# Windowed attention and a gated layer on one core: a change of order, of pairing and of the dilated heads' layout

## The chip, the core and the metric

The kernel runs on one core of a Trainium2 chip. The core has five engines that each take their own list of instructions in order: TensorE (PE) multiplies matrices into eight PSUM banks, VectorE (DVE), ScalarE (ACT) and GpSimd (POOL) work on elements, and SyncE (SP) issues transfers between memory and the core. An instruction that waits holds up all that stands behind it on its engine. The metric is the device time of one execution, in microseconds, lower is better.

## What is computed

```python
# q, k, v: 8 batches x 8 heads x 576 tokens x 64
scores = q @ k.T / sqrt(64)
mask_plain = (rel >= 0) & (rel < 32)                      # heads 0 to 3; rel = row - column
mask_dil   = (rel >= 0) & (rel < 128) & (rel % 4 == 0)    # heads 4 to 7
attn = softmax(where(mask, scores, -1e9)) @ v
x = attn with the heads side by side                      # 4608 tokens x 512
h = x @ w_in                                              # 512 x 1024
e = exp(h - max(h)); sm = e / sum(e); solu = h * sm
ln = (solu - mean) / sqrt(var + 1e-6) * g_ln
out = ln @ w_out                                          # 1024 x 512
```

## The kernel before

A unit is two heads of one batch (32 units, four to a batch; the third and fourth of each batch are dilated). The host puts the dilated heads' tokens class by class (token modulo 4), so that their mask becomes a plain window inside a class. For a unit n, the words `S` (scores, 72 small matmuls), `mask`, `max`, `sub`, `exp`, `sum`, `inv`, `norm` and `turn` make the transposed weights, and `V` multiplies them with the values into PSUM. `xh` (or `xf`) copies the result, rounded, into `x_hi`; `xl` (or `xd`) puts the rest into `x_lo`; where POOL forms the rest, `xc` first makes a plain copy for it. These copies put a dilated unit's tokens back into their order.

A tile is 128 tokens (36 tiles). Every product with `w_in` and `w_out` is done in two parts: high times high, high times low, low times high, so that one block of 128 rows costs three matmuls. For tile i the words `ha`, `hb` (left half of the columns) and `hc`, `hd` (right half) are six matmuls each; `ha` and `hc` need the units 0 and 1 of the batch, `hb` and `hd` the units 2 and 3. Then `peak` (DVE), `e` (ACT), `gate` (DVE), `mid`, `var` make the normalised row, `forth` and `back` send it through memory and back, `tr`, `th`, `tl` turn and split it, and `o` (24 matmuls; `oA` and `oB` are its halves) makes the output, `out` scales and stores it. The tiles' products with `w_in` stand in banks 0 and 1 or 2 and 3; the outputs of the early tiles in banks 0 and 1, which are free for them when the gate of tile 4 is done.

From tile `PAIRED` on two tiles go together: seven products `P1` to `P7` of six matmuls (42) take the place of eight blocks (48), with sums `z1` to `z4` of their inputs, and of the weights (`fa` to `fh`, then `Th`, `Tl`), made beforehand. `s` and `c` put the products together, `pk` finds the peak.

The two weight matrices come as 64-bit numbers, 16 blocks of 0.52 MB, and are turned into two rounded parts on the chip: for block b, `w` loads it, `field`, `low` and `sign` take the number apart, `join` puts it together, `hi` and `lo` make the two parts. Blocks 0 to 7 are `w_in`, 8 to 15 `w_out`; `hc` needs the blocks 1 and 3, `ha` 0 and 2, `hb` 4 and 6, `hd` 5 and 7.

The order is written out by hand: `OPENING` is a list of words, each of which issues its instructions on its engines; the loop after it does the same with `PAIR_BODY` for the last pairs. Each engine runs its own instructions in the order of that list. Tables say which engine does a step: `PE_MASK` (units whose mask is added by two matmuls of PE before the scores, line 307, rather than by DVE at line 337; these units' `sub` is on DVE, line 355, the others' on POOL, line 358), `POOL_NORM`, `DVE_LOW`, `ACT_CENTRE` (`mid` on ACT or DVE), `ZERO_SIGN` (`sign` on ACT or DVE), `ON_DVE` (`tl` and weight sums on DVE rather than POOL).

Of the kernel before, what the change touches and what calls it, by code (L numbers as in the profile page):

```python
# [21 lines left out]
NPAIR = H // 2  # L22
# [18 lines left out]
PE_MASK = (0, 1, 2, 3, 4, 5, 6, 7, 8, 9)  # L41
POOL_SUB = True
POOL_NORM = (0, 1, 2, 3, 4, 5, 6, 7, 8, 9, 10, 11, 12, 14, 15, 21, 22, 23, 25)
ACT_SCORES = ()
POOL_X = (2, 4, 5, 6, 9)
DVE_LOW = (0, 4, 8, 9, 10, 11, 12, 14, 15)
ACT_CENTRE = (0, 3, 4, 5, 7, 9, 10, 11, 14, 15, 20, 21)
# [3 lines left out]
ZERO_SIGN = (1, 2, 4, 5, 6, 8, 9, 10, 11, 12, 13, 14)  # L51
OPENING = (
# [87 lines left out]
def pair_words(r):  # L140
# [15 lines left out]
    "var.b tlA.a tlB.a out.d by.b tlA.b tlB.b oE.a out.a "  # L156
    "oE.b outE.b "
)
PAIRED = 12
SPLIT_UNIT = 16  # L160
POOL_WORDS = "z1 z2 z3 z4 lS12 lS34".split()
LOWEST = -3.4e38
# [12 lines left out]
def windowed_attention_then_solu_kernel(  # L175
# [70 lines left out]
    def buf(n):  # L246
        return n % 4 if n < 12 else n % 2
# [837 lines left out]
```

## Time and profile before

| | |
|---|---|
| median of three runs | 499.30 us (499.17 to 500.08) |
| profiled execution | 496.32 us |
| its span, first to last instruction | 494.5 us |
| PE busy | 461.7 us, 93% |
| DVE, ACT, POOL busy | 346.9, 306.6, 256.0 us |
| mean granted clock of TensorE | 0.997 |

The span is what the profile covers; 1.8 us of the execution lie outside it. PE is busy nearly throughout after the first 90 us; before, all of it, the loads, the conversion of the weights and the first units stand in each other's way. A matmul's end is modelled, so that PE's busy time in the opening contains waiting.

### The profile page before, as it was taken

The page shows a single profiled execution, that of the slowest core. Times are in us where ns is not written, and L with a number is a line of the kernel's source. Part 1 is how long each engine was busy: PE and PEld are TensorE (multiplying, and loading weights), DVE is VectorE, ACT ScalarE, POOL GpSimd, SP SyncE. Part 2 cuts the span into 40 slices and gives each one's busy share as a digit, 9 for nine tenths or more (in the row PEclk, how much of TensorE's full clock was granted, in tenths as well). Part 3 has the DMA queues.
Part 4 walks back from the last instruction along what each step waited for, and adds up shares of the span by engine and source line. Part 5 has one row for each costly group of instructions (what it writes and reads, how often), then busy time and mean ns, then how long its engine had stood idle before and what let it go on. Part 6 is the DMA issues. An engine that isn't in the chain of part 4 may idle for free.

```text
span 494.5 us, 15618 instructions
## 1 busy us (share of the span) xinstructions
PE 461.7 (93%) x6604; PEld 372.4 (75%) x6604; DVE 346.9 (70%) x622; ACT 306.6 (62%) x503; POOL 256.0 (52%) x334
## 2 busy tenths in 40 slices
PE   2469988899999899999999999999899999999996
PEld 1356766778887688788878888878688888888885
DVE  2867977877989467788959776867476754445472
ACT  4779877745652544574766666566566677667552
POOL 0245444734440546989448441676465656766420
PEclk9999999999999899999999999999999999999999
DMA  8978755774843435666488565866745545354452
GB/s 303 345 276 307 222 168 143 215 243 140 260 119 129 138 104 183 187 188 232 147 246 242 175 191 184 228 211 196 259 133 162 161 133 157 102 162 137 107 168 88
DMA packets 50902, 92.58 MB, mean 187 GB/s; under 512 B 5648, under 2 KB 25616, under 8 KB 50832
## 3 DMA queue, kind: packets, MB, share of 16 engines
q1 hardware_dynamic: 50112, 90.92, 59.1%
q8 instruction: 52, 0.85, 0.7%
q10 hardware_dynamic: 720, 0.66, 0.4%
q14 instruction: 18, 0.15, 0.1%
HBM read 58.53 MB, written 28.31 MB: 176 GB/s over the span
## 4 chain that ended last, share of the span: by engine, by line
PE 87%; DMA 4%; DVE 3%; ACT 3%; issue 2%; SPq 0%; POOL 0%; ACTq 0%; DVEq 0%
PE banks L597 38%; PE banks L826 24%; PE banks L467 12%; PE banks L398 6%; PE banks L319 5%; PE banks L632 2%; DMA tp<-w_in 2%; DMA qt<-qT 1%; DMA vt<-vw 1%; DVE x_lo L453 1%; SPq L255 0%; ACT e L518 0%; ACT e L493 0%; DVE mag L904 0%; DVE w_o L925 0%
## 5 line engine op out<-in xcount | busy, mean ns | idle before, releaser
L597 PE MATMUL banks<-w_o,th 128*128 128x512 f32 x544 | 169.2, 392 | 1.0 <-DVE mu L502 1.0
L597 PEld LDWEIGHTS banks<-w_o,th 128*128 128x128 f32 x544 | 101.2, 188 | 23.0 <-DVE mu L502 1.1
L597 PE MATMUL banks<-w_o,tl 128*128 128x512 f32 x272 | 106.1, 390 | 0.0
L467 PE MATMUL banks<-w_i,x_hi 128*128 128x512 f32 x192 | 63.6, 413 | 2.0 <-issue 2.0
L588 POOL TENSOR_TENSOR tl<-t,th 128x512 fp32r<-128x512 f32 x33 | 42.9, 1307 | 34.6 <-ACT th L582 34.5
L597 PEld LDWEIGHTS banks<-w_o,tl 128*128 128x128 f32 x272 | 51.0, 188 | 10.9
L582 ACT CAST th<-t 128x512 fp32r<-128x512 f32 x68 | 41.1, 619 | 18.4 <-DVE t L574 14.9
L850 DVE CUSTOM_DVE_ANT_0 t<-banks,t 128x512 f32<-128x512 f32 x36 | 24.5, 686 | 39.9 <-PE banks L826 33.0
L398 PEld LDWEIGHTS banks<-pt,vt 32*64 32x64 f32 x2624 | 34.6, 138 | 18.1 <-issue 9.2
L574 DVE STREAM_TRANSPOSE t<-raw 128x512 f32<-128x512 f32 x68 | 45.8, 692 | 2.3 <-ACT e L518 2.1
L398 PE MATMUL banks<-pt,vt 32*64 32x64 f32 (+1 forms) x2624 | 38.7, 238 | 9.2 <-issue 5.1
L467 PEld LDWEIGHTS banks<-w_i,x_hi 128*128 128x128 f32 x192 | 36.1, 194 | 10.2 <-issue 2.3
L511 ACT ACTIVATE t<-t,mu 128x1024 f32<-128x1024 f32 x26 | 30.0, 1154 | 21.0 <-DVE mu L510 20.5
L518 ACT ACTIVATE e<-t 128x1024 f32<-128x1024 f32 x35 | 37.0, 1058 | 5.0 <-DVE t L514 4.8
L467 PE MATMUL banks<-w_i,x_lo 128*128 128x512 f32 x96 | 38.6, 403 | 0.0
L377 POOL TENSOR_TENSOR sm<-sm,rs 128x576 f32<-128x576 f32 x19 | 22.7, 1196 | 30.4 <-DVE rs L372 29.6
L588 DVE TENSOR_TENSOR tl<-t,th 128x512 fp32r<-128x512 f32 x39 | 31.3, 815 | 9.8 <-ACT th L582 8.3
L358 POOL TENSOR_TENSOR sm<-sm,mx 128x576 f32<-128x576 f32 x22 | 28.1, 1284 | 18.9 <-DVE mx L345 12.7
L609 ACT ACTIVATE ob<-banks,rstd 128x512 f32<-128x512 f32 x35 | 23.9, 684 | 22.5 <-PE banks L597 12.1
L319 PEld LDWEIGHTS banks<-kt,qt 64*32 64x32 f32 x2304 | 27.0, 110 | 13.1 <-issue 10.4
L493 ACT ACTIVATE e<-t,nmax 128x1024 f32<-128x1024 f32 x23 | 26.5, 1152 | 16.6 <-DVE nmax L857 16.4
L319 PE MATMUL banks<-kt,qt 64*32 64x64 f32 x2304 | 32.9, 235 | 3.2 <-issue 3.2
(163 smaller groups left out, 927.6 us busy)
## 6 DMA issues: line engine op xcount, KB each, us to landing
mid<-t SPq DMA_DIRECT2D x140, 128.0 KB, 2.6
raw<-mid SPq DMA_DIRECT2D x34, 512.0 KB, 4.1
vt<-vw SPq DMA_DIRECT2D x32, 352.0 KB, 4.9
kt<-kT SPq DMA_DIRECT2D x32, 304.0 KB, 4.8
qt<-qT SPq DMA_DIRECT2D x32, 288.0 KB, 5.1
out<-ob SPq DMA_DIRECT2D x35, 256.0 KB, 2.8
x_hi<-x SPq DMA_DIRECT2D x12, 288.0 KB, 3.3
t<-w_in SPq DMA_DIRECT2D x5, 512.0 KB, 6.5
```

Of the source, the lines that this page charges most:

```text
L319: nc.tensor.matmul(out=ps[WIN * g : WIN * g + WIN, WQ * s0 : WQ * s0 + WQ], lhsT=qt[D * h : D * h + D, q0 : q0 + WIN], rhs=kt[D * h : D * ...
L358: eng.tensor_tensor(out=st[n]["sm"], in0=st[n]["sm"], in1=wide(mx), op=ALU.subtract)
L398: nc.tensor.matmul(out=ps_x[D * h : D * h + D, r // 2, c0 : c0 + k1 - k0], lhsT=vt[WIN * g : WIN * g + WIN, slot, :], rhs=pt[WIN * g : WIN ...
L467: nc.tensor.matmul(out=ps_h(i)[:, half], lhsT=a[:, kt, xs], rhs=w_i[:, kt, half, part, :], start=(kt == 0 and k == 0), stop=(kt == KT - 1 ...
L493: nc.scalar.activation(out=e, in_=h, func=AF.Exp, bias=nmax, scale=1.0, accum_out=se)
L511: nc.scalar.activation(out=dst, in_=src, func=AF.Identity, bias=mu, scale=1.0)
L518: nc.scalar.activation(out=e, in_=t, func=AF.Square, accum_out=per_tile(i, "sq"))
L574: nc.vector.transpose(out=turned(i)[:, cut(c)].rearrange("p k (a r) -> p k a r", r=WIN), in_=ms[i]["mv"].rearrange("p (a k s) -> p k a s", ...
L582: nc.scalar.copy(out=ms[i]["th"][:, cut(c)], in_=turned(i)[:, cut(c)])
L588: (nc.gpsimd if on_pool else nc.vector).tensor_tensor(out=ms[i]["tl"][:, cut(c)], in0=turned(i)[:, cut(c)], in1=ms[i]["th"][:, cut(c)].bit ...
L597: nc.tensor.matmul(out=ps_o(i), lhsT=a[:, f, :], rhs=w_o[:, f, part, :], start=(f == 0 and k == 0), stop=(f == FT - 1 and k == 2), skip_gr ...
L826: nc.tensor.matmul(out=banks[:, bank], lhsT=left(pa, kt), rhs=right(pb, kt), start=j in (1, 2, 5) and kt == 0 and k == 0, stop=kt == 1 and ...
```

## The change

Six things change; nothing else does.

- `PE_MASK` ends with unit 5: the masks of units 6 to 9 are added on DVE, and their `sub` goes to POOL, which is where the code puts it for all units without a mask on PE.
- `PAIRED` is 10: tiles 10 and 11 become a pair. From unit 10 on (before: 12) there are two buffers for queries, keys and values rather than four.
- For the dilated units the copies out of PSUM read in the order of the tokens (`p i a b`) and write contiguously; before, they read PSUM contiguously and wrote every fourth element.
- The words up to pair 12 stand in another order (the last 39 of `OPENING` and the loop after it keep theirs).
- `POOL_NORM`, `DVE_LOW`, `ACT_CENTRE`, `ZERO_SIGN`, `ON_DVE` move forty steps to other engines.
- The loop's rule for what is loaded ahead follows the fewer buffers.

```diff
-PE_MASK = (0, 1, 2, 3, 4, 5, 6, 7, 8, 9)
+PE_MASK = (0, 1, 2, 3, 4, 5)
-POOL_NORM = (0, 1, 2, 3, 4, 5, 6, 7, 8, 9, 10, 11, 12, 14, 15, 21, 22, 23, 25)
+POOL_NORM = (0, 1, 2, 3, 4, 5, 6, 7, 8, 10, 12, 15, 18, 21, 22)
-DVE_LOW = (0, 4, 8, 9, 10, 11, 12, 14, 15)
-ACT_CENTRE = (0, 3, 4, 5, 7, 9, 10, 11, 14, 15, 20, 21)
+DVE_LOW = (3, 4, 8, 9, 10, 11, 12, 14, 15)
+ACT_CENTRE = (0, 1, 2, 3, 4, 6, 8, 9, 10, 11, 13, 14, 15, 17, 19, 20, 21)
-ZERO_SIGN = (1, 2, 4, 5, 6, 8, 9, 10, 11, 12, 13, 14)
+ZERO_SIGN = (0, 2, 6, 7, 9, 11, 12, 13, 15)
 OPENING = (
-    "w1 q0 pack S0 low1 max0 q1 field1 w0 low0 sub0 exp0 sum0 w2 field2 sign1 q2 packd low2 inv0 S1 "
+    "w1 low1 w3 field3 low3 field1 sign1 join1 q0 sign3 join3 hi3 pack w0 low0 S0 max0 q1 v0 w2 "
...
-PAIRED = 12
+PAIRED = 10
...
     def buf(n):
-        return n % 4 if n < 12 else n % 2
+        return n % 4 if n < 10 else n % 2
...
     def x_order(n, x):
-        return x.rearrange("p (i a b) -> p a b i", a=2, b=2)
+        return x.rearrange("p (i a b) -> p i a b", a=2, b=2)
     def from_v(n):
-        return ps_x if n % NPAIR < NPAIR // 2 else ps_x.rearrange("p a (b i) -> p a b i", b=2)
+        return ps_x if n % NPAIR < NPAIR // 2 else ps_x.rearrange("p a (b i) -> p i a b", b=2)
...
-                if n in (10, 11):
+                if n in (6, 7):
-                n += 4 if n < 10 else 2
+                n += 4 if n < 6 else 2
```

How it moves instructions, at three places. First, SP's list at its start before; `t1` is the buffer of weight block 1, `t0` of block 0, `t2` of block 2, `kt0` and `qt0` hold unit 0's keys and queries, `packed` the plain mask:

```order
L255 DMA t1_103<-w_in 128x1024
L255 DMA kt0_106<-kT 128x608
L255 DMA qt0_105<-qT 128x576
L255 DMA packed_83<-pack 128x360
L255 DMA kt1_153<-kT 128x608
L255 DMA qt1_152<-qT 128x576
L255 DMA t0_158<-w_in 128x1024
L255 DMA t2_166<-w_in 128x1024
L255 DMA kt2_172<-kT 128x608
```

and after; `t3` is the buffer of weight block 3, `vt0` holds unit 0's values:

```order
L256 DMA t1_103<-w_in 128x1024
L256 DMA t3_107<-w_in 128x1024
L256 DMA kt0_118<-kT 128x608
L256 DMA qt0_117<-qT 128x576
L256 DMA packed_83<-pack 128x360
L256 DMA t0_125<-w_in 128x1024
L256 DMA kt1_170<-kT 128x608
L256 DMA qt1_169<-qT 128x576
L256 DMA vt0_173<-vw 128x704
```

Block 3 is now loaded ahead of the first unit's keys, and unit 0's values ahead of block 2 (before, they came fifteenth).

Second, ACT's list from its first conversion before; L883, L873 and L889 are `low`, `field` and `sign` of a weight block, L362 is an `exp`, L915 a `hi`:

```order
L883 ACTIVATE low1_148<-t1_103,below_86 128x512
L873 ACTIVATE mag1_156<-t1_103 128x512
L883 ACTIVATE low0_160<-t0_158,below_86 128x512
L362 ACTIVATE sm0_94<-sm0_94 128x9x64
L873 ACTIVATE mag2_168<-t2_166 128x512
L889 ACTIVATE low1_148<-t1_103 128x512
L883 ACTIVATE low2_176<-t2_166,below_86 128x512
L362 ACTIVATE sm1_95<-sm1_95 128x9x64
L889 ACTIVATE low2_176<-t2_166 128x512
```

and after (all lines are one higher):

```order
L884 ACTIVATE low1_105<-t1_103,below_86 128x512
L874 ACTIVATE mag3_109<-t3_107 128x512
L884 ACTIVATE low3_111<-t3_107,below_86 128x512
L874 ACTIVATE mag1_113<-t1_103 128x512
L916 CAST w_i_87<-mag3_109 128x512
L884 ACTIVATE low0_127<-t0_125,below_86 128x512
L363 ACTIVATE sm0_94<-sm0_94 128x9x64
L916 CAST w_i_87<-mag1_113 128x512
```

The blocks 1 and 3 (in `t1` and `t3`, those that `hc` needs) are now taken apart ahead of everything else, and the rounded part of block 3 is made before the first `exp`; before, block 1 was followed by the blocks 0 and 2, which `ha` needs, and by two `exp`s.

Third, DVE's list from the peak of tile 0 (L478) to that of tile 1 before; L502 is the gate, L904 a `join`, L345, L355, L366, L372 and L382 are `max`, `sub`, `sum`, `inv` and `turn`:

```order
L478 TENSOR_REDUCE nmax<-banks 128x1
L345 TENSOR_REDUCE mx<-banks 128x9
L382 STREAM_TRANSPOSE pt_798<-sm_94 128x576
L502 ISA t_801,mu<-banks,e 128x1024
L502 ISA mu 128x1
L510 TENSOR_SCALAR mu<-mu 128x1
L355 TENSOR_TENSOR sm_94<-banks,mx 128x9x64
L366 TENSOR_REDUCE rs<-sm_95 128x9
L904 SCALAR_TENSOR_TENSOR mag_729<-mag_729,low_734 128x512
L372 RECIPROCAL rs<-rs 128x9
L904 SCALAR_TENSOR_TENSOR mag_594<-mag_594,low_605 128x512
L478 TENSOR_REDUCE nmax<-banks 128x1
```

and after (all lines are one higher):

```order
L479 TENSOR_REDUCE nmax<-banks 128x1
L367 TENSOR_REDUCE rs<-sm_94 128x9
L905 SCALAR_TENSOR_TENSOR mag_627<-mag_627,low_650 128x512
L373 RECIPROCAL rs<-rs 128x9
L503 ISA t_785,mu<-banks,e 128x1024
L503 ISA mu 128x1
L511 TENSOR_SCALAR mu<-mu 128x1
L383 STREAM_TRANSPOSE pt_790<-sm_94 128x576
L338 TENSOR_TENSOR sm_94<-banks,dilated 128x9x64
L383 STREAM_TRANSPOSE pt_807<-sm_95 128x576
L346 TENSOR_REDUCE mx<-sm_94 128x9
L479 TENSOR_REDUCE nmax<-banks 128x1
```

A `sub` (L355) is gone and a mask (L338) has come in, two joins that stood between the peaks of tiles 0 and 1 are one, and two `turn`s stand where there was one.

## Rows read from the trace of the kernel before

**Rows 1.** chain that ended last, in order of time: start us, us, what
```profile
31.48 2.86 PE banks L467 x6
...
43.14 2.95 PE banks L467 x12
...
88.99 1.23 DVE t L502
90.28 11.21 PE banks L597 x48
...
114.65 1.06 PE banks L398 x55
...
160.31 2.13 issue
162.75 7.31 PE banks L467 x24
...
191.37 5.44 PE banks L597 x24
...
355.04 1.65 issue
```

**Rows 2.** busy time in a stretch: us, PE, PEld, DVE, ACT, POOL, PEclk, DMA share, GB/s
```profile
8.00:12.00 4.00, 2.36 (x122) 1.76 (x112) 2.04 (x3) 1.94 (x4) 0.00 (x0) 1.00 1.02 395
```

**Rows 3.** the same view, from the first peak to the first output
```profile
46.41:90.28 43.87, 38.79 (x893) 30.37 (x888) 37.54 (x60) 35.45 (x57) 22.03 (x36) 1.00 0.60 184
```

**Rows 4.** PE in order of time: start us, us, line, operation, idle before
```profile
7.20 0.66 PE L307 MATMUL banks<-packed 128*128 128x320 bf16 x2 [7.20 <-DMA packed<-pack]
7.80 1.34 PE L319 MATMUL banks<-kt,qt 64*32 64x64 f32 x72
...
23.91 0.68 PE L319 MATMUL banks<-kt,qt 64*32 64x64 f32 x31 [3.08 <-issue]
...
38.89 0.41 PE L307 MATMUL banks<-packed 128*128 128x320 bf16 x2 [1.01 <-DVE x_lo L453]
39.22 0.97 PE L319 MATMUL banks<-kt,qt 64*32 64x64 f32 x72
```

**Rows 5.** DVE groups by line and form: count, busy us, mean ns, idle before
```profile
L574 DVE STREAM_TRANSPOSE t<-raw 128x512 f32<-128x512 f32 x68 | 45.8, 692 | 2.3 <-ACT e L518 2.1 <-DMA raw<-mid 0.2
...
L382 DVE STREAM_TRANSPOSE pt<-sm 128x576 f32<-128x576 f32 x32 | 24.4, 766 | 4.0 <-POOL sm L377 3.9
L366 DVE TENSOR_REDUCE rs<-sm 128x9 f32<-128x585 f32 x32 | 24.1, 755 | 2.7 <-ACT sm L362 2.6
...
L502 DVE CUSTOM_DVE_ANT_0 t<-banks,e 128x1024 f32<-128x1024 f32 x12 | 14.6, 1216 | 5.9 <-ACT e L493 5.8
L478 DVE TENSOR_REDUCE nmax<-banks 128x1 f32<-128x1024 f32 x12 | 14.5, 1211 | 6.9 <-PE banks L467 6.9
...
L904 DVE SCALAR_TENSOR_TENSOR mag<-mag,low 128x512 int32<-128x512 int32 x16 | 10.8, 689 | 1.1 <-ACT mag L873 1.0
...
L337 DVE TENSOR_TENSOR sm<-banks,dilated 128x576 f32<-128x576 f32 x12 | 9.0, 753 | 8.9 <-ACT x L434 4.6 <-PE banks L319 3.0 <-PE banks L398 1.1
...
L514 DVE TENSOR_SCALAR t<-t,mu 128x1024 f32<-128x1024 f32 x10 | 8.0, 799 | 0.4
...
L355 DVE TENSOR_TENSOR sm<-banks,mx 128x576 f32<-128x576 f32 x10 | 7.6, 757 | 0.4
...
L925 DVE SCALAR_TENSOR_TENSOR w_o<-mag,packed,w_o 128x512 fp32r<-128x512 f32 x7 | 6.0, 871 | 0.0
```

**Rows 6.** line 436: duration ns min/median/max, first and last start
```profile
L436 ACT CAST x_hi<-banks x16: 610/912/1202, 20.7 to 189.8; 128x576 fp32r<-128x576 f32 x16
```

**Rows 7.** line 453: the same columns
```profile
L453 DVE TENSOR_TENSOR x_lo<-banks,x_hi x11: 690/1178/1228, 22.1 to 192.4; 128x576 fp32r<-128x576 f32 x11
```

**Rows 8.** DMA queues from 350 to 357 us: packets, MB, share of 16 engines
```profile
q1 hardware_dynamic: 1011, 2.39, 95.5%
q8 instruction: 1, 0.02, 0.9%
```

More of the change, by code (lines that the diff above doesn't have):

```diff
@@ L170 @@
 SHIFT = {}
-ON_DVE = ("tlA2", "tlB2", "tlA4", "tlA6", "fc0", "fb1", "fh0", "fa1", "fd1", "fc1", "tlB7", "fh1", "tlA9", "tlB9", "tlA10", "tlA11", "tlA12", "tlB14", "tlA16", "tlB16", "tlB17", "tlB18", "tlA18", "tlA19", "tlB3", "tlB4", "tlB5", "fd0", "tlA5", "tlA7", "fg1", "tlB10", "tlB11", "tlA13", "tlB13", "tlA14", "tlB19", "fe0", "fg0", "tlA8", "tlB15", "tlA17", "tlA3", "tlB6",)
+ON_DVE = ("tlA3", "tlB2", "fa0", "fb0", "fc0", "fh0", "fa1", "fc1", "fg1", "fh1", "tlB8", "tlA8", "tlA10", "tlA11", "tlB12", "tlA12", "tlB14", "tlA14", "tlB15", "tlA15", "tlB17", "tlA17", "tlA18", "tlB19", "tlA19", "tlB20", "fd0", "fb1", "fe1", "tlB5", "tlB7", "tlB6", "tlA9", "tlB10", "tlA13", "tlB13", "tlB16",)
 @with_exitstack
```

141 rows, old and new, of the table OPENING are left out of this document.

## The prediction

> **What bounds the kernel now.** I read the chain of waits in order of time first, to see where PE stops being the engine that ends last. From the first output product at 90.28 on [rows 1] the chain is PE's own work to the end, but for two gaps: 2.13 us at 160.31 and 1.65 us at 355.04, both "issue", in which PE waited for nothing that the profile shows. After the first, 24 matmuls took 7.31 us, where 24 take 5.44 elsewhere [rows 1], so that stall cost 2.13 + 1.87 = 4.0 us in all. A 128x512 matmul thus costs 5.44 / 24 = 0.227 us, and behind 90 us only fewer matmuls or fewer gaps can gain.
>
> Before 90 us it is different. The first block of a tile starts at 31.48, and the last block of tile 0 ends at 43.14 + 2.95 = 46.1 [rows 1]. The chain then passes through DVE, ACT and transfers until the gate of tile 4 ends at 88.99 + 1.23 = 90.2, which frees the banks of the first two outputs. From 46.41 to 90.28 [rows 3] DVE is busy 37.5 of 43.9 us, ACT 35.5, while PE has there some 37 us of work of its own (19 blocks of six matmuls, five units' scores at 0.97, four with a mask, and five value products at 1.06 [rows 1, 4]). So the opening is bound by two nearly full engines and by the order in which they work, and its first third by transfers as well (share 1.02 of the DMA engines, 395 GB/s [rows 2]).
>
> **The change part by part.**
>
> *Pairs from tile 10.* 48 matmuls become 42: 6 x 0.227 = 1.4 us off PE, in the stretch where PE sets the end, so all of it counts. The two tiles lose two peaks of 1.21 us on DVE and get four joins of products, and one more set of sums on POOL. What must be ready by then (sums of the weights) must be ready earlier. Between the first output and pair 5's first product PE has h6 to h9 and eight outputs (12 x 5.44), seven scores (0.97 each) and six value products (1.06 each): 78 us [rows 1, 4]. DVE's list has 75 instructions there, 57 us by single durations [rows 5], 73% of it. Before, it was 100 instructions and 78 us in the 106 us up to the first pair: 73% too. So I cost the earlier pair at nothing else; if the cover failed, PE would wait at the first product of pair 5.
>
> *Masks of units 6 to 9.* PE loses two matmuls a unit, 39.22 - 38.89 = 0.33 us [rows 4], 1.3 us in all, in the opening, where PE isn't last; I count nothing apart from the chain below. On DVE four masks of 0.753 take the place of four subtractions of 0.757 [rows 5]: nothing. POOL gets the four subtractions; each unit's `exp` then waits for POOL rather than DVE, behind other POOL work. The `norm` and `turn` of a unit come so much later, but its value product is due several words after; hidden, and half a microsecond a unit on DVE's waits if not.
>
> *Copies in token order.* An `x_hi` copy takes 0.610 us at least and 1.202 at most, an `x_lo` one 0.690 and 1.228 [rows 6, 7]; the forms differ only in the dilated units' stride of four elements on the writing side. If the side that is written sets the price, the new form costs 0.61 and 0.69; if a strided read of PSUM costs as much as a strided write did, it stays at 1.20 and 1.23; and it may be worse, with both heads' halves and both banks taken in turn. No row shows such a read. I take the lower end, since the read side has served every contiguous form at 0.61. In the opening, ACT saves 6 copies x 0.59 = 3.5 us (units 2, 3, 6, 7; two have a plain copy as well) and DVE 2 x 0.54. Of that only what PE waits for counts: `V3` waits for both copies of unit 2, `V7` for both of unit 6, 4 x 0.59 = 2.4 us; it is in the chain below.
>
> The Trainium skill bears on this (SBUF — State Buffer, "Door 1: The DMA port swizzle"): SBUF comes in lines of 16 bytes, and a pattern that meets a new line with each element pays. The 1.202 us of a 16-byte stride against 0.610 agree [rows 6]. The same passage gives PSUM lines of 8 bytes and says of strided patterns there that they slow matmuls; it speaks against the new read, and no run here shows one. By the first rule the copies halve, by the second they would not, which is the second rival.
>
> *The new order of the opening.* I work it out in two stretches.
>
> (1) To the end of tile 0's last block, before at 46.1. Block 3 (0.52 MB) is loaded ahead of unit 0: at 395 GB/s the scores start 1.3 us later, at 8.5 instead of 7.20, and last until 8.5 + 1.94 = 10.4 as before (7.20 to 7.80 + 1.34 [rows 4]). DVE then has, up to the rest of unit 1 (`xl1`), four maxima, four subtractions, three sums and three turns (11 x 0.755, a maximum taken as a sum, and 3 x 0.766), two joins (0.689), two rests (0.690), three reciprocals (about 0.2) and one weight rest (about 0.8): 10.6 + 1.4 + 1.4 + 0.6 + 0.8 = 14.8 us, and a wait for the first `exp`, some 0.7. So `xl1` at 26 and `V2` done at about 27.4. But before, PE stood still for 3.08 us inside `S3` without a visible cause, until 23.91 [rows 4], and the instructions ahead of it are the same in number. If that comes again, `V1` starts at 24.6, `xl1` ends at 27.5, `V2` at 29.1. Before, the first block began at 31.48. Five blocks, `V3`, `S4` and `S5` follow in both (5 x 1.36 + 1.06 + 2 x 1.30 = 10.5 us of PE); they took 46.1 - 31.5 = 14.6. With the same waits the new list ends them between 42.0 and 43.7; I take 43.0, which is 3.1 us ahead.
>
> (2) From there to the gate of tile 4. DVE's list before: 5 peaks (1.21), 5 gates (1.30 with the read of the sum), 12 maxima, sums and subtractions, 5 turns, 6 joins, 5 weight rests (0.87), 2 `mid` (0.95), 4 block transposes (0.69), one `x_lo` rest of 1.23, 4 reciprocals: 40.7 us by single durations [rows 5], done in 43.8. After: the same peaks, gates, turns, weight rests and reciprocals; masks in place of subtractions; 5 joins, 3 block transposes, a rest of 0.69, one `sign` (0.45), two weight sums (0.69), no `mid`: 38.7. At the same rate, 41.6 us. ACT's list in that stretch stays the same (45 instructions each), and ACT is ahead by six conversions and copies at its start. That is another 2.2 us, so the first output comes 5.3 us earlier, at 85. Without any wait of DVE it would be 8 or more; with all of the waits kept and the list only shifted, nothing. The remaining conversions (block 15) end some 5 us after the gate and are needed 5 us into the first output: as tight as before.
>
> *The rest of the new order and the forty moved steps.* Behind the first outputs DVE, ACT and POOL have slack, and PE hardly waited before; I cost these at nothing.
>
> Sum: 5.3 + 1.4 = 6.7 us off. The profiled execution took 496.32 (span 494.5 and 1.8 around it), 3.0 below the median of 499.30; I take the difference off the median: **492.6 us**.
>
> **The rivals.**
>
> *The opening keeps its length.* Both lists are nearly the same sums of work on two engines that are 81 and 86% busy [rows 3]; if DVE's waits move and don't go, only the pair is left: 499.3 - 1.4 = 498. For it: the lists differ by 2 us in 40. Against: the first block's inputs come earlier in the new list and ACT has 3.5 us less to do.
>
> *The copies don't get faster.* Then 2.4 us of the lead go: 495.0; with a still slower read (1.8 us) 497.4.
>
> *Slower: PE's supply of instructions.* Both gaps behind 90 us follow a unit's scores and a unit's value product that stand next to each other: 72 and 80-odd small matmuls, with as many weight loads, in 2 us. From 350 to 357 us the DMA engines were full (95.5%) and one packet of 16 KB of instructions passed [rows 8]. Before, 11 such neighbours stand behind the first output, and two of them were followed by a gap (4.0 and 1.65, 2.8 on the mean). In the new list there are 15. Three gaps more would cost 8.4 us: 501.0; from 2.4 more gaps on the change is a loss. Against it: nine of eleven passed without one.
>
> The Trainium skill says on this (Runtime: NRT & Kernel Launch, "Instruction fetch mechanics") that the sequencer fetches blocks of 256 instructions ahead and that this is mostly hidden. By that rule the neighbours cost nothing; the two gaps say otherwise for this kernel, or are something else.
>
> **How the numbers follow.** The forecast, 489 to 496 by itself, has 0.52; an opening shorter still (below 489) 0.03; slow copies 0.12; an opening of the old length 0.16; more gaps 0.17. The range is 486.5 to 500.8: it takes in the opening without DVE's waits and reaches into the last rival. Within 0.2% (498.3 to 500.3) a measurement of this kernel can't tell it from no change. Faster: 0.52 + 0.03 + 0.12 and half of 0.16: 0.75. The same: most of the other half and a little of the last: 0.09. Slower: 0.16.
>
> **What would show it.** The first output product should start at 83 to 87 us (before 90.28); tile 0's last block should end near 43. Lines 437 and 454 should show one duration, near 0.61 and 0.69, for all units. PE should have no gap at the first product of pair 5, and the number of "issue" gaps behind the first output should be two or three. PE's work behind the first output should be 1.4 us less. I am wrong if the first output starts after 89, if the copies still show 1.2 us, or if the gaps behind it add up to more than 10 us.

## The result and the profile after

The changed kernel takes **484.0 us** (median of four runs, 483.45 to 486.58) against 499.69 (499.17 to 500.32) in the same runs: a ratio of 0.9696, interval 0.9659 to 0.9733. That is 15.7 us off, where 6.7 were forecast, and below the range. Its lines are one higher than before (L597 is now L598).

The profiled execution took 486.58 us, 2.6 above its median; the one of before was 3.4 below this comparison's median. The profiles thus show 9.7 us of difference in span, and 6 of the 15.7 lie in executions of which no profile is shown. Page of after, part 1:

```profile
span 484.8 us, 15625 instructions
PE 457.4 (94%) x6590; PEld 371.8 (77%) x6590; DVE 350.0 (72%) x633; ACT 296.9 (61%) x502; POOL 283.1 (58%) x347
```

TensorE in order of time, after (start, duration, line, tile; in brackets idle time before and what ended it):

```profile
24.87 0.68 PE L320 MATMUL banks<-kt,qt 64*32 64x64 f32 x31 [3.10 <-issue]
...
47.77 0.35 PE L320 MATMUL banks<-kt,qt 64*32 64x64 f32 x16 [2.89 <-issue]
...
62.73 0.83 PE L399 MATMUL banks<-pt,vt 32*64 32x64 f32 x43 [2.06 <-issue]
63.49 1.22 PE L468 MATMUL banks<-w_i,x_hi 128*128 128x512 f32 x2
...
67.06 0.62 PE L468 MATMUL banks<-w_i,x_hi 128*128 128x512 f32 x2
...
88.76 0.62 PE L598 MATMUL banks<-w_o,th 128*128 128x512 f32 x2
...
168.36 0.39 PE L598 MATMUL banks<-w_o,tl 128*128 128x512 f32 x1
168.59 0.39 PE L827 MATMUL banks<-tp,w_i 128*128 128x512 f32 x1
...
470.00 1.07 PE L633 MATMUL banks<-w_o,th 128*128 128x512 f32 x4
```

and the start of the last outputs in before, the same view:

```profile
479.49 1.30 PE L632 MATMUL banks<-w_o,th 128*128 128x512 f32 x5
```

The first output starts 1.5 us earlier (88.76 against 90.28 [rows 1]), not 5.3. From it to the last outputs it is 470.00 - 88.76 = 381.2 us against 479.49 - 90.28 = 389.2: 8.0 less, where I had credited 1.4. So most of the time that the profiles show came out of the stretch whose order I had costed at nothing. TensorE's waits after (engine, tile, line, releaser: us in total, times, longest):

```profile
PE banks L308 <- DMA packed<-pack: 8.8, 1, 8.8
PE banks L320 <- issue: 6.0, 2, 3.1
PE banks L308 <- DVE sm L356: 3.5, 2, 1.9
PE banks L399 <- issue: 2.5, 2, 2.1
PE banks L399 <- DVE x_lo L454: 1.5, 1, 1.5
```

All four "issue" waits lie ahead of 63 us; the two behind the first output [rows 1] are gone, and with them the slow clock after the first of them. The one at 62.73 now costs the opening more than its 2.06: the granted clock fell from 1.00 to 0.76 and 0.81 in the stretches around it, which mixes the two levels (2.4 and 1.2 GHz), and two matmuls take 1.22 us at 63.49 and 0.62 at 67.06. Stretches of after (us; busy us and count of PE, PEld, DVE, ACT, POOL; clock; DMA share; GB/s):

```profile
43.64:88.76 45.12, 39.98 (x888) 31.52 (x887) 37.20 (x63) 36.05 (x58) 28.25 (x40) 0.96 0.62 190
...
56.00:60.00 4.00, 4.00 (x21) 3.03 (x19) 3.97 (x7) 3.89 (x7) 2.67 (x3) 1.00 0.84 332
...
61.00:65.00 4.00, 2.27 (x47) 1.92 (x48) 0.78 (x2) 1.88 (x4) 1.50 (x4) 0.76 0.04 8
65.00:69.00 4.00, 4.00 (x83) 3.07 (x82) 2.54 (x5) 3.20 (x6) 1.75 (x4) 0.81 0.56 129
```

The first row answers to [rows 3]: from the end of tile 0's last block, now 43.64, to the first output 45.1 us instead of 43.9, with DVE's and ACT's work nearly the same. The third shows the DMA engines idle (share 0.04) at the end of the gap at 62.73. That doesn't clear other transfers of it: they were busy until about its start (share 0.84, 332 GB/s in the second row). The copies, by line (least/median/largest ns, first and last start):

```profile
L437 ACT CAST x_hi<-banks x16: 618/638/643, 20.9 to 173.5; 128x576 fp32r<-128x576 f32 x16
...
L454 DVE TENSOR_TENSOR x_lo<-banks,x_hi x11: 696/744/758, 22.1 to 174.1; 128x576 fp32r<-128x576 f32 x11
```

### The profile page after: what moved, and what is told of

Read it like the earlier page. It is cut to its first block, busy times and chain, and to the rows that moved or that the text cites. A ratio compares the mean times of both kernels' runs of the same rounds, so it can differ in the third digit from the quotient of the medians.

```text
span 484.8 us, 15625 instructions
## 1 busy us (share of the span) xinstructions
PE 457.4 (94%) x6590; PEld 371.8 (77%) x6590; DVE 350.0 (72%) x633; ACT 296.9 (61%) x502; POOL 283.1 (58%) x347
## 4 chain that ended last, share of the span: by engine, by line
PE 48%; ACT 1%; POOL 1%; issue 0%; DVE 0%; ACTq 0%
PE banks L598 24%; PE banks L827 18%; PE banks L399 2%; PE banks L633 2%; PE banks L320 1%; ACT t L845 0%; POOL w_i L655 0%; ACT sm L363 0%; POOL sm L359 0%; DVE rs L367 0%; POOL kt L655 0%; DVE t L851 0%; ACT ob L647 0%; ACT w_i L785 0%; ACT x_lo L800 0%
## 5 line engine op out<-in xcount | busy, mean ns | idle before, releaser
L598 PE MATMUL banks<-w_o,th 128*128 128x512 f32 x544 | 168.9, 392 | 0.0
L598 PEld LDWEIGHTS banks<-w_o,th 128*128 128x128 f32 x544 | 101.5, 188 | 21.4
L598 PE MATMUL banks<-w_o,tl 128*128 128x512 f32 x272 | 106.1, 390 | 0.0
L589 POOL TENSOR_TENSOR tl<-t,th 128x512 fp32r<-128x512 f32 x40 | 55.2, 1385 | 36.8 <-ACT th L583 36.8
L851 DVE CUSTOM_DVE_ANT_0 t<-banks,t 128x512 f32<-128x512 f32 x39 | 26.6, 688 | 45.9 <-PE banks L827 40.4
L598 PEld LDWEIGHTS banks<-w_o,tl 128*128 128x128 f32 x272 | 51.1, 188 | 10.9
L468 PE MATMUL banks<-w_i,x_hi 128*128 128x512 f32 x160 | 53.0, 414 | 0.0
L359 POOL TENSOR_TENSOR sm<-sm,mx 128x576 f32<-128x576 f32 x26 | 33.4, 1283 | 31.1 <-DVE mx L346 31.0
L503 DVE CUSTOM_DVE_ANT_0 t<-t,e 128x1024 f32<-128x1024 f32 x25 | 32.0, 1278 | 15.2 <-ACT e L494 14.9
L845 ACT COPY t<-banks 128x512 f32<-128x512 f32 x39 | 22.6, 586 | 30.8 <-PE banks L827 20.0
L494 ACT ACTIVATE e<-t,nmax 128x1024 f32<-128x1024 f32 x25 | 28.8, 1150 | 20.8 <-DVE nmax L858 20.6
L468 PEld LDWEIGHTS banks<-w_i,x_hi 128*128 128x128 f32 x160 | 30.2, 196 | 6.6
L512 ACT ACTIVATE t<-t,mu 128x1024 f32<-128x1024 f32 x23 | 26.5, 1154 | 14.3 <-DVE mu L511 11.1
L378 POOL TENSOR_TENSOR sm<-sm,rs 128x576 f32<-128x576 f32 x15 | 18.4, 1227 | 26.9 <-ACT mag L874 14.3
```

The costliest lines, as they stand in the source:

```text
L359: eng.tensor_tensor(out=st[n]["sm"], in0=st[n]["sm"], in1=wide(mx), op=ALU.subtract)
L468: nc.tensor.matmul(out=ps_h(i)[:, half], lhsT=a[:, kt, xs], rhs=w_i[:, kt, half, part, :], start=(kt == 0 and k == 0), stop=(kt == KT - 1 ...
L494: nc.scalar.activation(out=e, in_=h, func=AF.Exp, bias=nmax, scale=1.0, accum_out=se)
L503: nc.vector.tensor_tensor_reduce(out=t, in0=h, in1=ms[i]["e"], scale=1.0, scalar=0.0, op0=ALU.mult, op1=ALU.add, accum_out=mu,)
L589: (nc.gpsimd if on_pool else nc.vector).tensor_tensor(out=ms[i]["tl"][:, cut(c)], in0=turned(i)[:, cut(c)], in1=ms[i]["th"][:, cut(c)].bit ...
L598: nc.tensor.matmul(out=ps_o(i), lhsT=a[:, f, :], rhs=w_o[:, f, part, :], start=(f == 0 and k == 0), stop=(f == FT - 1 and k == 2), skip_gr ...
```

## The experiments

**Theories.** By the first, the gain behind the first output is the new order's: its words wait less. By the second it is the copies'. The third came from the packets of the trace. At each "issue" gap over 0.3 us (74, counted over the fourteen profiles of this document, the runs below included) a 16 KB packet of instructions [rows 8] started between 2.3 us before TensorE stopped and 1.8 us after, and TensorE went on 2.2 to 3.1 us after the packet's start (2.45 at the median). A burst of small matmuls (a unit's scores next to a unit's value product, 304 to 316 instructions in 2 us, loads of weights counted too) can thus outrun the supply, and whether it does would depend on where in TensorE's stream it begins. If so, what counts is the place of each such pair modulo the length of the supplied piece, and any edit that shifts the stream moves every gap.

### Parts of the change

The kernel before with the copies alone, and the changed kernel with the old copies:

```diff
-        return x.rearrange("p (i a b) -> p a b i", a=2, b=2)
+        return x.rearrange("p (i a b) -> p i a b", a=2, b=2)
```

> The kernel before, with the dilated units' copies in token order and nothing else. My prediction priced these copies at 2.4 us of the opening: 497.3 us. If PE's work behind the first outputs and its gaps carry the change, the copies are worth little by themselves: 498.5 to 500. If the copies carry it: below 492. The copies themselves should show 0.61 to 0.65 us in every unit.

> The changed kernel with the strided copies of before put back and nothing else. By my prediction 2.4 us slower than the changed kernel: 486.4 us. If the copies matter only in the old order: 484. If they carry the change: 490 or more.

Measured: 495.97 us (ratio 0.9924, 0.9885 to 0.9962) and 486.17 (0.974, 0.9682 to 0.9797). The copies are worth 3.7 us in the one and 2.2 in the other: real, and a small part of 15.7.

Then the two halves of the order. The third kernel has the new words up to the second output (without the five sums of weights in them) and the old rest with pairs from 12; the fourth the old words up to there, masks on TensorE for units 0 to 9, and the new rest with pairs from 10; both have the new copies.

```diff
 # third kernel, against the changed one (the words, POOL_NORM, ACT_CENTRE and ON_DVE are left out here)
-PAIRED = 10
+PAIRED = 12
 # fourth kernel, against the changed one (the words and the other tables are left out here)
-PE_MASK = (0, 1, 2, 3, 4, 5)
+PE_MASK = (0, 1, 2, 3, 4, 5, 6, 7, 8, 9)
```

> The new order, new tables, masks of units 6 to 9 on DVE and token-order copies up to the first two outputs; behind them the old order, old tables and pairs from tile 12. By my prediction (the opening gains 5.3 us) 494.4 us. By the two traces, in which the first output starts only 1.5 us earlier, 497.5 to 498.5, the rest keeping its two gaps. If the opening carries the change: below 490.

> The old order, old tables and masks on PE up to the first two outputs, but token-order copies; behind them the new order, new tables and pairs from tile 10. By my prediction (only the pair gains there) 497 to 498 us. By the two traces, in which the stretch behind the first outputs is 7.7 us shorter: 488 to 492, with no gap of PE behind the first outputs.

Measured: 487.36 us (0.9767, 0.971 to 0.9824) and 489.2 (0.9819, 0.9742 to 0.9896). Each half takes nearly the whole gain, 12.3 and 10.5 us; with the copies, which both have, counted once (3.7), the halves would come to 12.3 + 10.5 - 3.7 = 19.1, more than the 15.7 they make together. The intervals are wide (about 3 and 4 us either way), so the excess is a hint and not shown. But the third kernel meets the number for an opening that carries the change (below 490), and the fourth the one for the rest (488 to 492). Both can't carry nearly all of it by their own words, and what they share must be looked for. Both shift TensorE's stream.

### The stream shifted

One-element matmuls ahead of the first word move all that follows; each is four TensorE instructions (two loads, two matmuls), and the first units wait for loads anyway.

```diff
+    for _ in range(9):    # 36 instructions; 64 make 256, 56 make 224
+        nc.tensor.matmul(out=banks[0:1, 7, 0:1], lhsT=mhalf, rhs=mhalf, ...)
```

> The changed kernel with nine 1x1 matmuls of a constant added at PE's start, before its first wait, 36 instructions that cost no time there. Theory (PE's gaps come where a block of 256 instructions lies so that it falls inside a unit's scores and the value product next to them): in the traces every pair of these that starts 130 to 160 instructions into a block of 256 shows a gap and no other does; the changed kernel has none there behind its first outputs, and the shift by 36 brings six. Each costs 1 to 4 us: 490 to 505 us, with gaps at these pairs. Rival (gaps come from full transfer queues, wherever the instructions lie): the same as the changed kernel, 484 us.

> The changed kernel with 64 such matmuls, 256 instructions: every pair keeps its place in its block. Both theories: the same as the changed kernel, 483 to 486 us, with no gap behind the first outputs. If the added matmuls cost something by themselves, it shows here.

> The kernel before with 56 such matmuls, 224 instructions, by which the four pairs with a gap (places 131, 156, 146 and 132 in their blocks) move to 99 to 124, and no pair lies between 125 and 170. Theory: the gaps at 160 and 355 us go, and those at 64 and 77 us with them: 490 to 494 us. Rival: the same as before, 498 to 500 us.

Measured: the changed kernel shifted by 36 takes **499.22 us** (0.9986, 0.9949 to 1.0024): the whole gain is gone, although every word, table and copy is the change's. Shifted by 256, seven times as much added work, it takes 485.32 (0.9724, 0.9666 to 0.9781), as unshifted. The kernel before shifted by 224 takes **489.72** (0.981, 0.9737 to 0.9884): 10.1 us off, with no part of the change. As a whole explanation, added work and the order both fall; the pieces are of 256 instructions or a divisor of 256 that 36 is not a multiple of (the places counted below leave only 256). In the profile of the shift by 36, five gaps of 0.3 to 2.9 us, 6.1 in all, stand behind the first output, at five pairs where six were expected, and from there to the last outputs it takes 391.1 us instead of 381.2. In that of the kernel before shifted by 224, the gaps at 64, 77, 160 and 355 us are gone, as expected, and one of 0.4 us has come. The Trainium skill says (Runtime: NRT & Kernel Launch, "Instruction fetch mechanics") that instructions are fetched in blocks of 256 and that this is mostly hidden. The period agrees with these runs; "mostly hidden" doesn't, for here it is worth 10 to 15 us of 499 (13.9 between the shifts by 36 and by 256, taken in the same comparison).

The same words in the changed kernel, unshifted, TensorE in order of time:

```profile
106.32 1.13 PE L399 MATMUL banks<-pt,vt 32*64 32x32 f32 x84
107.38 0.97 PE L320 MATMUL banks<-kt,qt 64*32 64x64 f32 x72
108.28 0.74 PE L598 MATMUL banks<-w_o,th 128*128 128x512 f32 x2
```

and shifted by 36 (lines five higher):

```profile
109.55 1.13 PE L404 MATMUL banks<-pt,vt 32*64 32x32 f32 x84
110.61 0.95 PE L325 MATMUL banks<-kt,qt 64*32 64x64 f32 x70
114.44 0.27 PE L325 MATMUL banks<-kt,qt 64*32 64x64 f32 x2 [2.88 <-issue]
114.64 0.73 PE L603 MATMUL banks<-w_o,th 128*128 128x512 f32 x2
...
116.50 1.06 PE L603 MATMUL banks<-w_o,th 128*128 128x512 f32 x2
```

The pair begins 103 instructions into its block in the first and 139 in the second, where it stops two matmuls short of its end for 2.88 us and the matmuls behind then run at half speed (two in 1.06 us). In the DMA queues of that kernel from 111.6 to 112.6 us, the first after TensorE stopped, stands one packet of instructions:

```profile
q1 hardware_dynamic: 84, 0.18, 97.8%
q8 instruction: 1, 0.02, 5.8%
```

and in the two us before, none:

```profile
q1 hardware_dynamic: 306, 0.64, 98.9%
```

The DMA engines were full in these two us and in the next, so that other transfers may have held the packet up here. They aren't needed for a gap. In the kernel before, one of the gaps that the shift by 224 took away came with the DMA engines idle from 72 to 76 us, and its packet started at 75.69 (TensorE after the gap, then that stretch):

```profile
77.89 0.32 PE L398 MATMUL banks<-pt,vt 32*64 32x32 f32 x8 [1.10 <-issue]
```

```profile
72.00:76.00 4.00, 3.66 (x106) 2.72 (x111) 1.23 (x3) 4.00 (x7) 2.32 (x4) 1.00 0.02 4
```

Counted over thirteen profiles, all but one of those told of here: of 240 pairs behind 50 us, 31 begin 120 to 159 instructions into a block of 256 (loads, matmuls and waits in the order of the trace), and 18 of those hold a gap or are followed by one within seven matmuls (over 0.7 us from one start to the next), 1.4 us of standing still on the mean; of the other 209, 6 are, three of them ended by VectorE. A place there makes a gap likely, not sure.

The traces also show where in a block TensorE stops, and it is one place only: each of the 74 gaps ends before the instruction 193 or 194 into a block of this count, in every kernel and at every shift. (The count starts with the first instruction of the trace; the pieces evidently start some instructions earlier.) A profile has 51 or 52 of the packets, one for each 256 instructions, and in 711 passages of that point, with a gap or without, TensorE was never there less than 2.17 us after the start of the packet for it. A pair that begins at 120 to 159 passes the point early, and again 256 instructions on, near its own end. At 305 instructions in 2 us that is 1.7 us later, an estimate: less than the packet takes, so that TensorE stops there unless the packet started ahead of the first passage.

When the packet starts goes with the other traffic too. Behind 50 us in the thirteen profiles, packets started 0.9 us after the passage before theirs, at the median, where the DMA engines were less than 0.2 busy in the microsecond ahead, and 1.55 us after it where they were at least 0.95 busy. Of the 29 gaps there (again over 0.7 us from one start to the next), 8 came with the first and 12 with the second. Full transfer queues can add to a gap; they are not the whole cause.

### The order of the words in the opening

> The changed kernel with five words that sum the weights for the pairs (two on DVE ahead of the gate of tile 4) moved behind the first two outputs. In the hybrid with the new opening and the old rest these words stood later, and its first output started 3.3 us earlier. If DVE's list is what the first output waits for: first output 1 to 3 us earlier, 481 to 483 us. If the earlier start came from one PE gap less in that one execution: 484 us.

```diff
 # five sums of the weights moved behind the second output (... stands for words that stay)
-... "hb4 hd4 fb0 v8 low15" ... "e4 fa0 lo12" ... "forth4 fc0 fd0 fe0 trA2 e5 xl8 v9 o0 gate5 o1 thA2"
+... "hb4 hd4 v8 low15" ... "e4 lo12" ... "forth4 trA2 e5 xl8 v9 o0 gate5 o1 fb0 fa0 fc0 fd0 fe0 thA2"
```

Measured: 486.72 us (0.9756, 0.97 to 0.9813), not the 481 to 483 expected. The first output comes at 87.45 instead of 88.76, and three waits for VectorE behind it, of 0.5 to 1.2 us, which the changed kernel doesn't have, take that back. Here the order is worth 1 to 2 us either way.

### What is left when the place is good

Places chosen by such a count over the runs up to here: the changed kernel with 62 one-element matmuls (248), the kernel before with the copies and 224, and, as a test that could fail, the worst place for the changed kernel (60).

> The kernel after the change with 62 one-element matmuls of TensorE ahead of its first word: 248 of its instructions (a load of weights and a matmul count one each, four for each of these matmuls in float32), which is 8 less than a whole block of 256. Only the place of its stream in blocks of 256 changes. Theory of the place: a scores-and-values pair costs a stall of 1 to 3 us where it begins 125 to 180 instructions into a block; here one of the pairs behind the first outputs stands there (at 172), none of the opening's. So 482 to 486 us, at most one gap behind the first outputs, and as fast as the changed kernel or up to 2 us faster. Rival (any shift that is not a whole block costs, as the one by 36 did): 494 to 500 us.

> The kernel before the change with 224 of TensorE's instructions ahead of it, as in the run of that shift (489.7 us), and with the dilated heads' values written in token order as well. Theory (what is left of the gain beside the place in the blocks is in part the copies): 2 to 3.5 us less than with the shift alone, 486 to 488 us. Rival (the copies stand beside TensorE's work, and their 3.7 us in the first run of them were a shift of the gaps): 489 to 491 us.

> The kernel after the change with 15 such matmuls ahead: 60 instructions. By the theory of the place this is the worst shift for this order of words: seven scores-and-values pairs behind the first outputs begin between 136 and 174 in their block (at 106, 127, 171, 216, 283, 320 and 344 us of the changed kernel's profile). At the 1.7 us that six such gaps took on average in the run shifted by 36 instructions: 484 + 7 x 1.7 = 496 us, in a range of 492 to 503, and gaps of 0.7 to 3 us at most of those seven pairs and at no others. Rival (the run shifted by 36 was slow for another reason, such as a lower clock): 484 to 487 us with no gaps behind the first outputs, or gaps at other pairs.

Measured: 485.09 us (0.972, 0.9666 to 0.9774; three runs, 482.86 to 486.01), **485.19** (0.9729, 0.9683 to 0.9775; a little under the 486 to 488 expected) and 500.26 (1.0005, 0.9968 to 1.0041). The first's profile was taken at a mean granted clock of 0.673, so nothing of its pace is read. The time at the worst place came as expected (492 to 503), but not by the path expected, so that part is luck: of the seven pairs named only three had gaps in its profile, 3.4 us together. That profile is of the fastest of its ten runs (495.83), and it took 384.9 us from the first output to the last ones, 3.7 more than the changed kernel's; 5.4 were lost ahead of the first output, at 94.19, where no loss had been forecast and two gaps took 4.1 and 4.3. TensorE's waits of that kernel:

```profile
PE banks L325 <- issue: 9.1, 4, 4.1
PE banks L404 <- issue: 7.8, 3, 4.3
```

The second says most: the kernel **before**, with new copies and its stream 224 further on, is within 1.2 us of the changed kernel, with intervals that overlap, without the new order, the earlier pair or the moved masks. First and last outputs of the kernel shifted by 224 alone, then with the copies:

```profile
88.41 0.72 PE L602 MATMUL banks<-w_o,th 128*128 128x512 f32 x2 [0.95 <-DVE mu L507]
...
472.35 0.84 PE L637 MATMUL banks<-w_o,th 128*128 128x512 f32 x3
```

```profile
84.73 0.72 PE L602 MATMUL banks<-w_o,th 128*128 128x512 f32 x2
...
468.70 0.84 PE L637 MATMUL banks<-w_o,th 128*128 128x512 f32 x3
```

With the copies the first output comes 3.7 us earlier; from there on it is 383.9 and 384.0 us. Their price by form, in the same order:

```profile
L441 ACT CAST x_hi<-banks 128x576 fp32r<-128x576 f32 x16 | 14.6, 915 | 11.0 <-PE banks L403 6.6 <-DVE sm L342 4.3
```

```profile
L441 ACT CAST x_hi<-banks 128x576 fp32r<-128x576 f32 x16 | 10.2, 635 | 12.0 <-PE banks L403 7.7 <-DVE sm L342 4.3
```

Last, the fourth kernel (old opening, new rest) at that shift, as a candidate for the fastest:

```diff
+    for _ in range(56):    # ahead of the fourth kernel's first word
```

> The kernel with the opening of before, its masks on TensorE and both parts that the earlier runs left of the change (token-order copies, and everything from the first output on as in the changed kernel, with the pairs from tile 10), and 224 of TensorE's instructions ahead of it. By the place in the blocks its opening has no bad pair any more (131 becomes 99, 156 becomes 124) and of the pairs behind it only the last, at 162, is one. Theory (the opening's words and the masks give nothing of their own; the pair gives 1.4 us): 1 to 3 us under the 485.2 us of the kernel before with token copies at this shift, 482 to 484.5 us, as fast as the changed kernel or faster. Rival (the new opening is needed for the changed kernel's 484.0 us): 486 to 489 us.

Measured: 486.99 us (0.9771, 0.9726 to 0.9816). It beats neither; the numbers expected were missed by 2.5 us, and the rival's (486 to 489) were met. Its trace says where:

```profile
74.93 0.65 PE L324 MATMUL banks<-kt,qt 64*32 64x64 f32 x40 [1.75 <-issue]
...
88.59 0.73 PE L602 MATMUL banks<-w_o,th 128*128 128x512 f32 x2
...
469.72 0.84 PE L637 MATMUL banks<-w_o,th 128*128 128x512 f32 x3
```

Behind the first output it takes 381.1 us, like the changed kernel (381.2) and 2.8 less than the old rest with one gap of 0.4 us (383.9). But the opening that ended at 84.73 ends at 88.59 here, with a gap of 1.75 inside a pair that begins 124 instructions into its block, a place that had none in the run before; its packet started only 5.2 us after the passage before it, with the DMA engines full. I took the opening's 84.73 for a property of its words; it isn't. Nor does the rival follow, that the new opening is needed: this profile (486.29) and the changed kernel's (486.58) have their first output at 88.59 and 88.76 and are alike behind it, and the 3 us between the medians stand in no profile. Over the profiles with the new copies, those shifted by 36 and 60 left out, the first output came at 85.4 to 88.8 us with the new opening and at 84.7 to 89.7 with the old: one order is not shown to be faster than the other. No version tried is faster than the changed kernel.

## Why the prediction was wrong, step by step

- **"The rest of the new order and the forty moved steps": "I cost these at nothing."** This is the step that failed. The words themselves are worth little: with no gap in the new rest and one of 0.4 us in the old, it takes 381.1 us for 383.9, 2.8 less, and my estimate of the pair is 1.4 of it. What I had not costed is that they move TensorE's stream against its pieces of 256 instructions. In the profiles that is 389.2 - 383.9 = 5.3 us behind the first output (about what I had worked out for the two gaps, 4.0 + 1.65 [rows 1]); in the times, 10.1 us for the kernel before and 15.2 for the changed one.
- **The rival "PE's supply of instructions"** had the mechanism and the wrong rule. I counted neighbours (11 before, 15 after; the traces have 13 and 17) and so made it a loss of 8.4 us; what decides is where each begins. The numbers for a better rule were in the trace before: all of its seven gaps over 0.3 us end before the instruction 193 or 194 of a block, and there are pairs with and without a gap to compare. My forecast then held the gaps to be as many as before, with no reason for it.
- **The opening, 5.3 us.** 1.5 came in the profile. The first stretch ended at 43.64 (43.0 forecast). The second took 45.1 us instead of the 41.6 that I put on it. One term was mis-sized: I had DVE's work there fall by 2.0 us, from 40.7 to 38.7, and the profiles have 37.5 [rows 3] and 37.2, a fall of 0.3. Two gaps, 2.89 and 2.06 us, and the slow clock behind the second stand in the same stretch; how much of its length is theirs is not shown. That the list alone would give 85 isn't either: the third kernel, with the new words less five, had its first output at 85.44, and the old list with new copies once at 84.73 and once at 88.59.
- **The copies: right.** One duration, 0.638 and 0.744 at the median [rows 6, 7], and 3.7 us on the path against the 2.4 that I put there. That is about all six copies that ACT does faster in the opening (3.5 us by my count) rather than four; which of them counted is not shown. The strided read of PSUM costs nothing extra for ACT or DVE (single copies take 0.618 to 0.643 and 0.696 to 0.758 us, the same for both kinds of unit): the doubt that I took from the Trainium skill (SBUF — State Buffer, "Door 1: The DMA port swizzle"), whose remark on strided PSUM is on matmuls, does not carry to these copies, while its 16-byte lines agree with 1.20 us for the strided write [rows 6].
- **The pair: its cover held.** Its first product follows the output before it at 168.59 without a wait. Its 1.4 us was not run by itself and is not shown; it would be a part of the 2.8 us of the new rest.
- **The masks at nothing:** not tried alone; the old masks are in the fourth kernel, which stays within 3 us of the changed one at a good place.

What stays open: what sets the start of a packet, which in some passages came ahead of the passage before it and in others 5 us behind it, so that a given place stalls in one run and not in the next; and the 6 us between the profiles' difference and that of the medians. Times of before went from 495.2 to 502.4 us in the comparisons, those of the kernel at its good place with the copies from 484.88 to 485.40. That gaps differ from run to run would explain both; one profile a kernel doesn't show it. The 0.2% within which I held a measurement to be no change was too small for such a spread.

## What to carry to other kernels

Where one engine is 94% busy and a trace shows gaps on it that nothing releases, with a packet of instructions at each, count whether they all end at the same instruction of 256, and try the kernel shifted by some tens of one-element instructions before crediting any new order: here 36 of them cost the changed kernel 15 us, as much as the whole change gave, and 224 took 10 us off the kernel before. When two halves of a change each give nearly the whole of it, look for what both displace. Compare orders at the best shift of each, or the place of the stream is taken for the order's merit.

## What the runs showed of the hardware

- A gap of TensorE that ends with "issue" came with a 16 KB packet on the instruction queue: 74 gaps over 0.3 us in fourteen profiles, all before the same instruction of 256, give or take one, none ended less than 2.17 us after its packet's start. They came with the DMA engines idle (share 0.02 from 72 to 76 us of the kernel before, ahead of a gap of 1.10) and full (98.9% from 109.6 to 111.6 us of the changed one shifted by 36).
- The same 313 small instructions cost nothing at 103 instructions into a block and 2.88 us at 139; a shift by a whole 256 changed nothing (485.3 us for 484.0), one by 36 cost 15.2 us, one by 60 16.3.
- A gap can cost twice: behind one of 2.06 us the granted clock was 0.76 from 61 to 65 us, and the matmuls behind took 1.22 us for two instead of 0.62.
- A copy that reads PSUM with a stride and writes contiguously costs ACT 0.638 us, like a plain one; written with a stride it cost 1.202 [rows 6].
